# Weight sums and splits one conversion step later, and the last gated output's splits spread over rational steps

## Chip, cores and metric

One core of one Trainium2 chip. The metric is the device time of one execution in microseconds (us): median 962.09 of three runs of the kernel before (962.02 to 962.68).

## What is computed

Inputs and outputs are float32; the weights arrive as 64-bit floats and the kernel turns their bits into float32 itself.

```python
x = attention(q, k, v)               # 2304 tokens x 512, windowed and global
gate = 1.0 / (1.0 + np.exp(-(x @ w_gate)))
val = x @ w_val                      # d_ff 1536
y = gate * val @ w_out
h = y @ w_in                         # d_ff 2048
P = a[0] + a[1] * h + a[2] * h**2 + a[3] * h**3
Q = 1.0 + np.abs(b[0]) * np.abs(h) + np.abs(b[1]) * h**2
out = (P / (Q + 1e-06)) @ w_out2
```

## The kernel before

Three stages follow each other on the core: attention up to about 126 us, the gated layer to about 578 us, the rational layer to the end. Every float32 product is three TensorE matmuls: each operand is split into a high part (a cast on ScalarE) and a low part (a subtraction, on GpSimd for weights), names with `h` and `l`. The 2304 tokens are four tiles of 512 (numbers 0 to 3) and one of 128 (number 4, `glob`); the hidden features come in blocks `f` of 128, twelve of them in the gated layer.

**The passes.** The gated layer first takes tiles 0, 1 and glob in six passes p = 0 to 5, two blocks each (p = 3 takes blocks 6 and 7). In a pass TensorE makes the gate and value products of tile 0, tile 1 and glob (`pg`, `pv`, lines 713 to 715) and the output products (`p`, 831 to 833); at the end glob's gated product is transposed (`turn`, line 785) and split into `gh_glob` (ScalarE, 759) and `gl_glob` (VectorE, 764), and `second_glob` (793 to 799) multiplies both with the output weights: two blocks, lines 797 and 798 with `gh_glob`, 799 with `gl_glob`, each twice. The next pass starts right behind on TensorE.

**The conversion beside it.** During the passes `Weights` converts weights that later parts want, piece by piece, in one order of pieces numbered j: for each block its two gate/value pieces (`v18gv` is block 8 of the gated layer, and there are two of that name; `v19gv` is block 9), for each block an output piece, and pieces of the rational layer (`v20out`, `v21out`, `v20in`; the first digit is the layer). Piece j passes five steps: `magnitude` (ScalarE, two ACTIVATEs, 566 and 567), `bits` (VectorE, three operations, 574 to 576), `add` (GpSimd, 583), `hi` (ScalarE, 605), `lo` (GpSimd, 613), then `keep` writes the result to DRAM (SyncE, 597). `bits` also issues the load of piece j + 3. Three staging buffers `st` of one kind serve all pieces of the rational layer and the sums below.

**The sums.** Tiles 2 and 3 are done after the passes (385 to 567 us) by a Strassen scheme, `strassen`, which wants sums of the weight blocks: `combine` makes them of the two gate/value pieces of a block: 631 (VectorE), 632 (GpSimd), 634 and 636 (VectorE), then two splits (642 on ScalarE, 643 on GpSimd) into two staging buffers, and four writes to DRAM.

**What sets the order.** `Weights.__init__` writes a list per pass, `plan`, of steps with a cost (0.7 or 0.6); `Pace` hands them out between the pieces of TensorE's work in `gated` (919 to 960) until a pass's share is spent. For each j the list has magnitude(j), bits and add of j - 1, hi and lo of j - 2, and, where piece j - 2 was the second of a block, the four parts of `combine` right behind. Each engine works its queue in the order in which the program issues.

**The transition.** The last output products of tiles 2 and 3 (`second` with `final` set) give each m of four a VectorE sum (`gacc`, 845) and at once its split: `yh` (ScalarE, 848) and `yl` (849, GpSimd for m = 0 and 2, VectorE for 1 and 3). The rational layer's pipeline runs over units (unit 0 to 3: tile 0, 4 to 7: tile 2, later tile 3); step n of its loop issues `first` of unit n (`rp`, TensorE 713 to 715), `quad` (GpSimd, 1160) and, for older units, `quot` (VectorE, 1193), `hi` (`rgh`, ScalarE 1202), `lo` (`rgl`, GpSimd 1214) and `second` (TensorE 1243 to 1245, unit n - 4). It calls `before` (the `rest` that `gated` returns) at n = 1 and n = 2; the first call issues tile 2's last output products with their splits, the second tile 3's and then `back(1)`, the loads of tile 1's parked outputs. The table of ln and exp for ScalarE is loaded ahead of the first step (line 1124).

Of the kernel before, what the change touches and what calls it, by code (L numbers as in the profile page):

```python
# [8 lines left out]
F32 = mybir.dt.float32  # L9
# [440 lines left out]
class Weights:  # L450
# [10 lines left out]
    def __init__(self, tc, early, dram, ins, outs):  # L461
# [30 lines left out]
        for p in range(len(ends) - 1):  # L492
            out = []
            last = p == len(ends) - 2
            for j in range(ends[p], ends[p + 1] + (2 if last else 0)):
                for back, steps in ((0, (self.magnitude,)), (1, (self.bits, self.add)), (2, (self.hi, self.lo))):
                    i = j - back
                    if ends[0] <= i < len(self.order):
                        out += [(0.7, step, i) for step in steps]
                        if back == 2 and self.order[i][0] == 1 and self.order[i][2:] == ("gv", 1):  # L500
                            out += [(0.6, self.combine, self.order[i][1], n) for n in range(4)]
# [123 lines left out]
    def combine(self, f, i):  # L625

        nc = self.nc
        v0, v1 = (self.whole[1, f, "gv", k] for k in range(2))
        g0, a0, g1, a1 = v0[:, 0:256], v0[:, 256:512], v1[:, 0:256], v1[:, 256:512]
        if i == 0:  # L630
            nc.vector.tensor_tensor(a1, a0, a1, ALU.add)
            nc.gpsimd.tensor_tensor(a0, g0, a0, ALU.subtract)
        elif i == 1:
            nc.vector.tensor_tensor(g0, a1, g0, ALU.subtract)
        elif i == 2:
            nc.vector.tensor_tensor(g1, g1, g0, ALU.subtract)
        for src, names, turn in ((v0, ("s2", "s3"), 2), (v1, ("s4", "s1"), 3)):
            if i == turn:
                t = self.stage(f"{f}{names[0]}")
                h, l = self.parts(t)  # L640
                src = src.rearrange("p (x c) -> p x c", x=2)
                nc.scalar.copy(h, src)
                nc.gpsimd.tensor_tensor(l, src, h.bitcast(F32), ALU.subtract)
                for x, name in enumerate(names):
                    self.keep((1, f, name, 0), t[:, x * 512 : x * 512 + 512])
# [90 lines left out]
def gated(nc, pools, only, xpool, dram, wp, ident, xh, xl):  # L736
# [85 lines left out]
    def second(f0, i, gs, half):  # L822
# [17 lines left out]
        for m in ms:  # L840
# [5 lines left out]
            if final:  # L846
# [9 lines left out]
                if i > 1:  # L856
                    park(yh[i][:, m], yl[i][:, m])
                else:
                    parks.append(away)
# [250 lines left out]
    def rest():  # L1110
        for _ in range(2):
            queue.pop(0)()
        if not queue:
            back(1)
        wp.pump(len(wp.loads))
# [4 lines left out]
def rational(nc, pools, rest, wp, ident, xh, xl, before, co, out):  # L1120
# [3 lines left out]
    nc.scalar.preload_act_table_set("natural_log_exp_and_others")  # L1124
# [149 lines left out]
    for n in range(len(units) + 8):  # L1274
# [119 lines left out]
```

## Time and profile before

| | |
|---|---|
| median of 3 runs | 962.09 us |
| the profiled execution | 961.38 us, of which the span (first to last instruction) is 959.5 us |
| TensorE busy | 907.8 us (95%) |
| VectorE busy | 753.1 us (78%) |
| ScalarE busy | 581.4 us (61%) |
| GpSimd busy | 572.1 us (60%) |
| mean granted TensorE clock | 0.977 of full speed |

Times in the profile count from the start of the span. PE is TensorE (matmuls), DVE VectorE, ACT ScalarE, POOL GpSimd, SP SyncE. The mean duration of an instruction is what the profiler shows; matmuls overlap, so one that shows 0.39 us starts 0.23 us behind the one before at full clock. A busy share is a mean over stages that differ, so the stages are looked at apart: passes (about 126 to 385 us), Strassen part, transition (566 to 602 us). Idle time of an engine is charged to what ended last before it went on.

### The profile page before, as it was taken

How to read it: one execution, taken by the hardware profiler on the slowest of the kernel's cores; microseconds unless marked ns; L12 is line 12 of the kernel's file. 1: busy time of each engine (PE TensorE's matmuls, PEld its weight loads, DVE VectorE, ACT ScalarE, POOL GpSimd, SP SyncE). 2: the span in 40 equal slices, each digit the busy share in tenths (PEclk: the TensorE clock that was granted, in tenths of full speed). 3: DMA queues.
4: the chain of work that ended last, by engine and by line, in shares of the span. 5: the costliest groups of instructions: out<-in, count | busy, mean ns of one | idle time of the engine just before them, and what ended most of it. 6: DMA issues, size and time to landing. Idle time of an engine off the chain costs nothing.

```text
span 959.5 us, 13769 instructions
## 1 busy us (share of the span) xinstructions
PE 907.8 (95%) x4666; PEld 749.0 (78%) x4666; DVE 753.1 (78%) x1355; ACT 581.4 (61%) x1161; POOL 572.1 (60%) x470
## 2 busy tenths in 40 slices
PE   7989999959797979999999997999999999999998
PEld 6778888848585857788888786888888888888886
DVE  6988885777676777686776848977788889888887
ACT  6978964444444444334444346777777778777673
POOL 4766866657565657346666655635465667566564
PEclk9999999979897989999999999999999999999999
DMA  9755265666565667578989792002200310020112
GB/s 303 235 198 152 78 242 183 239 215 230 192 237 192 225 219 285 208 272 294 328 318 331 268 362 74 0 1 90 86 1 1 111 66 1 1 88 1 45 55 88
DMA packets 60805, 156.24 MB, mean 163 GB/s; under 512 B 7104, under 2 KB 9152, under 8 KB 60736
## 3 DMA queue, kind: packets, MB, share of 16 engines
q1 hardware_dynamic: 60640, 155.24, 46.5%
q8 instruction: 37, 0.61, 0.3%
q14 instruction: 32, 0.26, 0.1%
q10 hardware_dynamic: 96, 0.13, 0.1%
HBM read 103.17 MB, written 52.17 MB: 162 GB/s over the span
## 4 chain that ended last, share of the span: by engine, by line
PE 72%; DVE 13%; POOL 5%; DMA 4%; issue 3%; ACT 2%; SPq 1%; POOLq 0%; DVEq 0%; ACTq 0%
PE rp L1245 6%; PE rp L1243 6%; PE rp L1244 6%; PE rp L715 6%; PE rp L713 6%; PE rp L714 6%; PE p L833 2%; PE p L832 2%; PE p L831 2%; PE pair L261 2%; PE pg L713 2%; PE pg L714 2%; PE pg L715 1%; PE bank L380 1%; PE pv L715 1%
## 5 line engine op out<-in xcount | busy, mean ns | idle before, releaser
L1160 POOL TENSOR_TENSOR v<-v,u 128x512 f32<-128x512 f32 x68 | 91.0, 1338 | 110.5 <-ACT v L1156 110.5
L1214 POOL TENSOR_TENSOR rgl<-t,rgh 128x512 fp32r<-128x512 f32 x64 | 89.9, 1405 | 40.6 <-POOL v L1160 18.8
L1168 DVE TENSOR_TENSOR t<-rp,t 128x512 f32<-128x512 f32 x68 | 46.8, 688 | 45.0 <-ACT t L1164 43.9
L295 POOL TENSOR_TENSOR p<-p,r 128x448 f32<-128x448 f32 x64 | 58.7, 941 | 36.7 <-DVE r L290 24.2
L1153 ACT ACTIVATE u<-rp 128x512 f32<-128x512 f32 x68 | 40.5, 596 | 63.8 <-PE rp L715 60.2
L1193 DVE SCALAR_TENSOR_TENSOR t<-t,co,v 128x512 f32<-128x512 f32 x68 | 72.9, 1072 | 2.4
L1189 DVE SCALAR_TENSOR_TENSOR v<-v,u 128x512 f32<-128x512 f32 x68 | 74.7, 1098 | 0.0
L759 ACT CAST gh<-t 128x512 fp32r<-128x512 f32 x38 | 23.6, 620 | 73.3 <-DVE t L752 64.4
L280 ACT ACTIVATE p<-p,mx 128x224 f32<-128x224 f32 x128 | 60.2, 479 | 7.8 <-DVE mx L272 7.8
L1185 DVE SCALAR_TENSOR_TENSOR v<-v,u 128x512 f32<-128x512 f32 x68 | 59.1, 869 | 1.1 <-ACT u L1181 1.1
L845 DVE TENSOR_TENSOR gacc<-p,gacc 128x512 f32<-128x512 f32 x80 | 51.5, 681 | 10.4 <-PE p L833 10.3
L1156 ACT ACTIVATE v<-u,co 128x512 f32<-128x512 f32 x68 | 55.6, 817 | 2.3
L764 DVE TENSOR_TENSOR gl<-t,gh 128x512 fp32r<-128x512 f32 x38 | 35.5, 934 | 27.2 <-ACT gh L759 27.2
L1177 ACT ACTIVATE u<-v,co 128x512 f32<-128x512 f32 x68 | 49.2, 724 | 6.7 <-POOL v L1160 6.7
L1164 ACT ACTIVATE t<-rp,co 128x512 f32<-128x512 f32 x68 | 51.8, 761 | 0.5 <-POOL rgl L1214 0.5
L1172 DVE SCALAR_TENSOR_TENSOR t<-t,co,rp 128x512 f32<-128x512 f32 x68 | 50.2, 738 | 0.0
L1181 ACT ACTIVATE u<-u,co 128x512 f32<-128x512 f32 x68 | 48.5, 713 | 2.3 <-DVE t L1168 2.2
L1202 ACT CAST rgh<-t 128x512 fp32r<-128x512 f32 x64 | 39.0, 610 | 15.4 <-DVE t L1193 15.4
L272 DVE CUSTOM_DVE_ANT_0 p<-pair,masks 128x224 f32<-128x224 f32 x128 | 42.1, 383 | 7.0 <-DMA masks<-in_masks 6.3
L752 DVE TENSOR_TENSOR t<-pv,t 128x512 f32<-128x512 f32 x28 | 19.2, 685 | 25.8 <-PE pv L715 24.5
L1268 POOL TENSOR_TENSOR racc<-ev,racc 128x512 f32<-128x512 f32 x22 | 37.9, 1743 | 0.0
L261 PE MATMUL pair<-kn,qn 64*128 64x224 f32 x256 | 30.2, 368 | 2.3 <-ACT pgn L319 1.2
(1388 smaller groups left out, 3199.9 us busy)
## 6 DMA issues: line engine op xcount, KB each, us to landing
raw1gv<-in_w_gate_val SPq DMA_DIRECT2D x24, 512.0 KB, 3.7
raw2in<-in_w_in SPq DMA_DIRECT2D x16, 512.0 KB, 4.3
raw2out<-in_w_out SPq DMA_DIRECT2D x16, 512.0 KB, 3.8
kn<-in_k_l SPq DMA_DIRECT2D x15, 448.0 KB, 5.4
raw1out<-in_w_out SPq DMA_DIRECT2D x12, 512.0 KB, 3.6
vn<-in_v_l SPq DMA_DIRECT2D x16, 256.0 KB, 3.8
out<-racc SPq DMA_DIRECT2D x16, 256.0 KB, 2.0
qn<-in_q_l SPq DMA_DIRECT2D x15, 256.0 KB, 4.7
```

The costliest lines, as they stand in the source:

```text
L280: nc.scalar.activation(p, p, AF.Exp, bias=s["mx", half][:, n : n + 1], scale=-1.0, accum_out=s["sm", half][:, n, 0:1])
L295: nc.gpsimd.tensor_tensor(p, p, r, ALU.mult)
L713: nc.tensor.matmul(ps, wh, mh[:, k], start=k == 0, stop=False)
L714: nc.tensor.matmul(ps, wh, ml[:, k], start=False, stop=False)
L715: nc.tensor.matmul(ps, wl, mh[:, k], start=False, stop=k == 3)
L1160: nc.gpsimd.tensor_tensor(s["v"], s["v"], s["u"], ALU.mult)
L1185: nc.vector.scalar_tensor_tensor(s["v"], s["v"], Q_CONST, s["u"], ALU.add, ALU.mult)
L1189: nc.vector.scalar_tensor_tensor(s["v"], s["v"], 2.0, s["u"], ALU.subtract, ALU.mult)
L1193: nc.vector.scalar_tensor_tensor(s["t1"], s["t1"], a0, s["v"], ALU.add, ALU.mult)
L1214: nc.gpsimd.tensor_tensor(s["gl"], s["t1"], s["gh"].bitcast(F32), ALU.subtract)
L1243: nc.tensor.matmul(ps, gh[:, w], wh, start=k == 0, stop=False)
L1244: nc.tensor.matmul(ps, gh[:, w], wl, start=False, stop=False)
```

## The change

Three edits. In the plan of a pass, for each j, hi(j - 2) now comes first, then magnitude(j), bits(j - 1), lo(j - 2), add(j - 1); `combine` is cut in two, `sums` (the four additions) which follows piece j - 3 and `splits` (the two splits with their writes) which follows piece j - 4, each handed out as one item of cost 1.2. In the transition the splits of the last outputs of tiles 2 and 3 are put on the list `parks` instead of being issued; `rest(n)` issues tile 2's output products at n = 1, its four splits at n = 2, tile 3's products at n = 3 and its splits at n = 4 and 5, with `back(1)` at 5. The load of the ln/exp table moves from ahead of the first step to n = 1. The number of instructions stays; lines shift by one (to line 847) and by four or more behind it.

```diff
--- before.py
+++ after.py
@@ -493,12 +493,11 @@
             out = []
             last = p == len(ends) - 2
             for j in range(ends[p], ends[p + 1] + (2 if last else 0)):
-                for back, steps in ((0, (self.magnitude,)), (1, (self.bits, self.add)), (2, (self.hi, self.lo))):
+                for back, steps in ((2, (self.hi,)), (0, (self.magnitude,)), (1, (self.bits,)), (2, (self.lo,)), (1, (self.add,)),
+                                    (3, (self.sums,)), (4, (self.splits,))):
                     i = j - back
-                    if ends[0] <= i < len(self.order):
-                        out += [(0.7, step, i) for step in steps]
-                        if back == 2 and self.order[i][0] == 1 and self.order[i][2:] == ("gv", 1):
-                            out += [(0.6, self.combine, self.order[i][1], n) for n in range(4)]
+                    if ends[0] <= i < len(self.order) and (back < 3 or self.order[i][0] == 1 and self.order[i][2:] == ("gv", 1)):
+                        out += [(1.2 if back > 2 else 0.7, step, i) for step in steps]
             self.plan.append(out)
 
 
@@ -622,27 +621,27 @@
         elif j >= self.EARLY:
             self.keep(key, t)
 
-    def combine(self, f, i):
-
-        nc = self.nc
+    def sums(self, j):
+
+        nc, f = self.nc, self.order[j][1]
         v0, v1 = (self.whole[1, f, "gv", k] for k in range(2))
         g0, a0, g1, a1 = v0[:, 0:256], v0[:, 256:512], v1[:, 0:256], v1[:, 256:512]
-        if i == 0:
-            nc.vector.tensor_tensor(a1, a0, a1, ALU.add)
-            nc.gpsimd.tensor_tensor(a0, g0, a0, ALU.subtract)
-        elif i == 1:
-            nc.vector.tensor_tensor(g0, a1, g0, ALU.subtract)
-        elif i == 2:
-            nc.vector.tensor_tensor(g1, g1, g0, ALU.subtract)
-        for src, names, turn in ((v0, ("s2", "s3"), 2), (v1, ("s4", "s1"), 3)):
-            if i == turn:
-                t = self.stage(f"{f}{names[0]}")
-                h, l = self.parts(t)
-                src = src.rearrange("p (x c) -> p x c", x=2)
-                nc.scalar.copy(h, src)
-                nc.gpsimd.tensor_tensor(l, src, h.bitcast(F32), ALU.subtract)
-                for x, name in enumerate(names):
-                    self.keep((1, f, name, 0), t[:, x * 512 : x * 512 + 512])
+        nc.vector.tensor_tensor(a1, a0, a1, ALU.add)
+        nc.gpsimd.tensor_tensor(a0, g0, a0, ALU.subtract)
+        nc.vector.tensor_tensor(g0, a1, g0, ALU.subtract)
+        nc.vector.tensor_tensor(g1, g1, g0, ALU.subtract)
+
+    def splits(self, j):
+
+        nc, f = self.nc, self.order[j][1]
+        for k, names in enumerate((("s2", "s3"), ("s4", "s1"))):
+            t = self.stage(f"{f}{names[0]}")
+            h, l = self.parts(t)
+            src = self.whole[1, f, "gv", k].rearrange("p (x c) -> p x c", x=2)
+            nc.scalar.copy(h, src)
+            nc.gpsimd.tensor_tensor(l, src, h.bitcast(F32), ALU.subtract)
+            for x, name in enumerate(names):
+                self.keep((1, f, name, 0), t[:, x * 512 : x * 512 + 512])
 
     def allow(self, n):
         self.limit += n
@@ -853,10 +852,7 @@
                     park(t[:, 0:512], t[:, 512:1024])
                     wp.keep((9, i, "y", m), t)
 
-                if i > 1:
-                    park(yh[i][:, m], yl[i][:, m])
-                else:
-                    parks.append(away)
+                parks.append((lambda m=m, park=park: park(yh[i][:, m], yl[i][:, m])) if i > 1 else away)
         if half == 1 and i in (1, 3):
             for g in range(G):
                 wp.release((1, f0 + g, "out", 0))
@@ -1107,12 +1103,13 @@
         step()
     pace.finish()
 
-    def rest():
-        for _ in range(2):
+    def rest(n):
+        for _ in range({1: 2, 3: 2}.get(n, 0)):
             queue.pop(0)()
-        if not queue:
+        for _ in range({2: 4, 4: 2, 5: 2}.get(n, 0)):
+            parks.pop(0)()
+        if n == 5:
             back(1)
-        wp.pump(len(wp.loads))
 
     return yh, yl, rest
 
@@ -1121,7 +1118,6 @@
     G = G2
     NF = FF2 // 128
     acc = [None] * len(TILES)
-    nc.scalar.preload_act_table_set("natural_log_exp_and_others")
     nc.vector.tensor_scalar_mul(co[:, 0:4], co[:, 0:4], -1.0)
     nc.scalar.activation(co[:, 4:6], co[:, 4:6], AF.Abs)
     nc.vector.memset(co[:, 6:7], Q_CONST * LN_SCALE)
@@ -1272,6 +1268,8 @@
     steps = dict(first=first, abs=abs_, lin=lin, quad=quad, p3=p3, p2=p2, p1=p1, log=log, exp=exp, r1=r1, r2=r2,
                  quot=quot, hi=hi, lo=lo, second=second, out=evacuate)
     for n in range(len(units) + 8):
+        if n == 1:
+            nc.scalar.preload_act_table_set("natural_log_exp_and_others")
         for name, ahead, *args in PLAN2:
             u = n + ahead
             if name in ("second", "out") and u >= LATER:
@@ -1286,8 +1284,7 @@
                 if i == LAST_TURNS[-1] and name == "first" and fs[0] % G == G - 1:
                     for k in range(4):
                         wp.release((2, fs[0] - G + 1, "in", k))
-        if n in (1, 2):
-            before()
+        before(n)
         wp.pump(len(wp.loads))
```

How the instructions move, at three places.

ScalarE at the end of pass 3, where `gh_glob` stands (`hi` of a piece is a CAST at 605 before, 604 now; splits of sums are `st8s`, `st9s`); before:

```order
L605 CAST w19gv_0_3147<-v19gv_2977 128x2x256
L566 ACTIVATE v21out_3152<-raw2out_3048 128x512
L567 ACTIVATE q21out_3153<-raw2out_3048 128x512
L605 CAST w19gv_0_3162<-v19gv_3041 128x2x256
L642 CAST st9s_3189<-v19gv_2977 128x2x256
L642 CAST st9s_3196<-v19gv_3041 128x2x256
L566 ACTIVATE v18out_3203<-raw1out_3111 128x512
L567 ACTIVATE q18out_3204<-raw1out_3111 128x512
L605 CAST st20out_3229<-v20out_3104 128x512
L759 CAST gh_glob<-pt_3231 128x256
```

and now:

```order
L604 CAST w19gv_0_3138<-v19gv_3043 128x2x256
L565 ACTIVATE v21out_3140<-raw2out_3050 128x512
L566 ACTIVATE q21out_3141<-raw2out_3050 128x512
L641 CAST st8s_3155<-v18gv_2933 128x2x256
L641 CAST st8s_3162<-v18gv_2948 128x2x256
L604 CAST st20out_3185<-v20out_3060 128x512
L565 ACTIVATE v18out_3187<-raw1out_3095 128x512
L566 ACTIVATE q18out_3188<-raw1out_3095 128x512
L604 CAST st21out_3220<-v21out_3140 128x512
L758 CAST gh_glob<-pt_3222 128x256
```

Between the last `w19gv` cast and `gh_glob` stood block 9's two sums splits; now block 8's stand there, and the cast `st21out`, which stood behind `gh_glob`, is ahead of it.

GpSimd in the same stretch (583 and 582 are `add`, 613 and 612 `lo`, 632 and 630 the sums' subtraction, 643 and 642 the splits); before:

```order
L613 TENSOR_TENSOR w19gv_0_3147<-v19gv_2977,w19gv_0_3147 128x2x256
L583 TENSOR_TENSOR v20out_3104<-v20out_3104,q20out_3105 128x512
L613 TENSOR_TENSOR w19gv_0_3162<-v19gv_3041,w19gv_0_3162 128x2x256
L632 TENSOR_TENSOR v19gv_2977<-v19gv_2977 128x256
L643 TENSOR_TENSOR st9s_3189<-v19gv_2977,st9s_3189 128x2x256
L643 TENSOR_TENSOR st9s_3196<-v19gv_3041,st9s_3196 128x2x256
L583 TENSOR_TENSOR v21out_3152<-v21out_3152,q21out_3153 128x512
L613 TENSOR_TENSOR st20out_3229<-v20out_3104,st20out_3229 128x512
L583 TENSOR_TENSOR v18out_3203<-v18out_3203,q18out_3204 128x512
L613 TENSOR_TENSOR st21out_3292<-v21out_3152,st21out_3292 128x512
```

and now:

```order
L630 TENSOR_TENSOR v18gv_2933<-v18gv_2933 128x256
L612 TENSOR_TENSOR w19gv_0_3138<-v19gv_3043,w19gv_0_3138 128x2x256
L582 TENSOR_TENSOR v20out_3060<-v20out_3060,q20out_3061 128x512
L642 TENSOR_TENSOR st8s_3155<-v18gv_2933,st8s_3155 128x2x256
L642 TENSOR_TENSOR st8s_3162<-v18gv_2948,st8s_3162 128x2x256
L612 TENSOR_TENSOR st20out_3185<-v20out_3060,st20out_3185 128x512
L582 TENSOR_TENSOR v21out_3140<-v21out_3140,q21out_3141 128x512
L630 TENSOR_TENSOR v19gv_2995<-v19gv_2995 128x256
L612 TENSOR_TENSOR st21out_3220<-v21out_3140,st21out_3220 128x512
L582 TENSOR_TENSOR v18out_3187<-v18out_3187,q18out_3188 128x512
L642 TENSOR_TENSOR st9s_3283<-v19gv_2995,st9s_3283 128x2x256
```

The subtraction of block 8's sums now comes behind the add of `v19gv`, its splits behind the add of `v20out`; the add of `v21out`, which the cast `st21out` needs, comes behind these splits and the `lo` of `st20out`; block 9's splits go to the next pass.

GpSimd at the transition, from the first rational `quad` on; before:

```order
L1160 TENSOR_TENSOR v_5756<-v_5756,u_5754 128x512
L1160 TENSOR_TENSOR v_5779<-v_5779,u_5777 128x512
L849 TENSOR_TENSOR yl_5802<-gacc_4266,yh_5801 128x512 x2
L1160 TENSOR_TENSOR v_5848<-v_5848,u_5846 128x512
L849 TENSOR_TENSOR yl_5874<-gacc_4421,yh_5873 128x512 x2
L1214 TENSOR_TENSOR rgl_5855<-t_5758,rgh_5854 128x512
L1160 TENSOR_TENSOR v_5935<-v_5935,u_5933 128x512
```

and now:

```order
L1156 TENSOR_TENSOR v_5755<-v_5755,u_5753 128x512
L1156 TENSOR_TENSOR v_5779<-v_5779,u_5777 128x512
L1156 TENSOR_TENSOR v_5840<-v_5840,u_5838 128x512
L848 TENSOR_TENSOR yl_5802<-gacc_4266,yh_5801 128x512 x2
L1210 TENSOR_TENSOR rgl_5847<-t_5757,rgh_5846 128x512
L1156 TENSOR_TENSOR v_5879<-v_5879,u_5877 128x512
L1210 TENSOR_TENSOR rgl_5886<-t_5781,rgh_5885 128x512
L1156 TENSOR_TENSOR v_5948<-v_5948,u_5946 128x512
L848 TENSOR_TENSOR yl_5905<-gacc_4421,yh_5904 128x512
L1210 TENSOR_TENSOR rgl_5971<-t_5842,rgh_5970 128x512
```

Tile 3's two splits (`yl_5874`) stood ahead of the first `rgl`; now only tile 2's two do, and tile 3's (`yl_5905`) come behind the second `rgl`.

## Rows read from the trace of the kernel before

**Rows 1.** Windows: PE, PEld, DVE, ACT, POOL busy (count); granted clock; DMA share; GB/s.
```profile
265.00:305.00 40.00, 33.45 (x146) 27.04 (x145) 28.33 (x42) 16.99 (x31) 25.52 (x21) 0.87 0.64 224
...
385.00:425.00 40.00, 39.97 (x177) 32.71 (x178) 29.44 (x37) 14.06 (x25) 16.39 (x12) 1.00 0.61 220
580.00:620.00 40.00, 35.09 (x148) 28.54 (x147) 37.69 (x45) 29.95 (x48) 22.46 (x16) 0.96 0.09 27
```

**Rows 2.** Waits of PE over the whole span: us in total, times, longest.
```profile
PE p_glob L797 <- ACT gh_glob L759: 27.8, 4, 9.5
PE rp L1245 <- POOL rgl L1214: 4.9, 1, 4.9
```

**Rows 3.** Timeline of PE, ends of passes 1, 3, 5: start, duration, instruction, [idle before <- releaser].
```profile
204.31 0.79 PE L799 MATMUL p_glob<-w12out,gl_glob 128*128 128x512 f32 x1 [0.47 <-DVE gl_glob L764]
...
295.05 0.79 PE L797 MATMUL p_glob<-w16out,gh_glob 128*128 128x512 f32 x1 [6.08 <-ACT gh_glob L759]
...
296.73 0.80 PE L799 MATMUL p_glob<-w16out,gl_glob 128*128 128x512 f32 x1 [0.46 <-DVE gl_glob L764]
...
298.61 0.63 PE L713 MATMUL pg<-xh,w18gv 128*128 128x512 f32 x1
...
385.03 0.50 PE L799 MATMUL p_glob<-w110out,gl_glob 128*128 128x512 f32 x1 [2.27 <-DVE gl_glob L764]
```

**Rows 4.** Windows right behind three waits of PE, for the granted clock.
```profile
298.50:302.00 3.50, 3.50 (x10) 2.66 (x10) 3.03 (x5) 1.76 (x3) 0.75 (x2) 0.51 0.61 241
385.00:388.00 3.00, 2.97 (x13) 2.48 (x14) 2.31 (x3) 1.14 (x2) 2.03 (x2) 1.00 0.93 373
595.00:598.00 3.00, 2.97 (x8) 2.33 (x9) 2.96 (x4) 2.14 (x4) 1.72 (x2) 0.58 0.03 5
```

**Rows 5.** Timeline of ACT at the end of pass 3.
```profile
291.94 1.14 ACT L642 CAST st9s<-v19gv 128x512 fp32r<-128x512 f32 x2 [5.56 <-DVE v19gv L634]
...
294.63 0.37 ACT L759 CAST gh_glob<-pt 128x256 fp32r<-128x256 f32 x1
```

**Rows 6.** Timeline of DVE in pass 3.
```profile
273.78 0.69 DVE L576 SCALAR_TENSOR_TENSOR v19gv<-raw1gv,v19gv 128x512 uint32<-128x512 uint32 x1
...
278.74 0.42 DVE L752 TENSOR_TENSOR t_glob<-pgv,t_glob 128x256 f32<-128x256 f32 x1
...
286.44 0.43 DVE L575 TENSOR_SCALAR v20out<-v20out 128x512 uint32<-128x512 uint32 x1
...
294.24 1.38 DVE L575 TENSOR_SCALAR v21out<-v21out 128x512 uint32<-128x512 uint32 x1
...
296.26 0.42 DVE L764 TENSOR_TENSOR gl_glob<-pt,gh_glob 128x256 fp32r<-128x256 f32 x1
```

**Rows 7.** Timeline of POOL in pass 3.
```profile
279.55 2.86 POOL L643 TENSOR_TENSOR st8s<-v18gv,st8s 128x512 fp32r<-128x512 f32 x2 [1.19 <-ACT st8s L642]
...
287.67 1.30 POOL L583 TENSOR_TENSOR v20out<-v20out,q20out 128x512 uint32<-128x512 uint32 x1 [1.55 <-PE pv L715]
...
290.73 0.72 POOL L632 TENSOR_TENSOR v19gv<-v19gv 128x256 f32<-128x256 f32 x1 [0.54 <-DMA raw1out<-in_w_out]
```

**Rows 8.** Timeline of PE at the transition.
```profile
595.03 0.50 PE L1245 MATMUL rp<-w20out,rgl 128*128 128x512 f32 x1 [4.91 <-POOL rgl L1214]
```

**Rows 9.** Timeline of ACT at the transition.
```profile
568.63 1.28 ACT L1124 ACT_TABLE_LOAD   x1
...
586.36 0.62 ACT L1202 CAST rgh<-t 128x512 fp32r<-128x512 f32 x1 [1.08 <-DVE t L1193]
...
591.34 1.22 ACT L848 CAST yh<-gacc 128x512 fp32r<-128x512 f32 x2 [1.96 <-DVE gacc L845]
```

**Rows 10.** Timeline of POOL at the transition.
```profile
592.03 1.27 POOL L849 TENSOR_TENSOR yl<-gacc,yh 128x512 fp32r<-128x512 f32 x1 [1.88 <-ACT yh L848]
593.26 1.72 POOL L1214 TENSOR_TENSOR rgl<-t,rgh 128x512 fp32r<-128x512 f32 x1
```

**Rows 11.** Timeline of DVE at the transition.
```profile
584.66 1.67 DVE L1193 SCALAR_TENSOR_TENSOR t<-t,co,v 128x512 f32<-128x512 f32 x1
```

## Prediction

> **What bounds the kernel now.** First the windows by stage. In the Strassen part TensorE is busy 39.97 of 40 us at full clock; in a pass only 33.45 of 40, at a granted clock of 0.87, and around the transition 35.09 [rows 1]. No other engine is full in the passes (DVE 28.33, POOL 25.52), so TensorE waits there for a chain of short steps, not for a busy engine. Second, the waits of TensorE: 27.8 us for `gh_glob` in four passes and 4.9 us for the first `rgl` [rows 2]; at most a few us elsewhere. Third, what each wait costs besides itself: behind 6.08 us of waiting for `gh_glob`, the 3.5 us from 298.5 show a clock of 0.51 (its lower level, 1.2 GHz) and 10 matmuls, while the 3 us behind the 2.27 us wait at 385.03 show 1.00 (2.4 GHz) and 13; behind the 4.91 us wait at the transition it is 0.58 and 8 in 3 us [rows 3, 4]. So a long wait costs about two us more than it lasts, and a wait of 2.27 us nothing more.
>
> Fourth, what `gh_glob` waits for. On ScalarE it starts at 294.63 without idle time ahead: the splits `st9s` came at 291.94 after 5.56 us of waiting for the sums of block 9, then two ACTIVATEs and the cast `st20out` [rows 5]. The sums wait for GpSimd's subtraction at 290.73, which stands behind the add of `v20out` (287.67) and a `lo` [rows 7]. `gl_glob` is 296.26, behind the bits of `v21out` on VectorE [rows 6], and releases line 799 at 296.73 [rows 3]. From line 799 on TensorE has no more waits, so the start of 799 sets where the next pass begins.
>
> **Part 1, the plan of the passes.** It removes no instruction; per pass the same steps are issued, the writes to DRAM and loads included. What I walk is the order of the change in pass 3 with durations of the rows, from a point that both orders share: the end of bits of the first `v19gv`, 273.78 + 0.69 = 274.5 [rows 6].
> - Now the add of this piece (1.3, as 287.67 [rows 7]) ends at 275.8, the cast 0.5 and magnitude(`v20out`) 1.15 behind it stand ahead of glob's sigmoid, and VectorE's `t_glob` starts at 277.9, against 278.74 [rows 6]: 0.8 earlier, since no sums stand ahead of it.
> - Then bits of the second `v19gv`, 1.6 with GpSimd idle; `t_1` and `gl_1` with the cast between, 2.0; sums of block 8, 0.42 + 0.73 + 0.8 with the subtraction between [rows 7]; bits of `v20out`, 2.5: they end at 286.4 instead of 287.6, 1.2 earlier.
> - GpSimd: add 1.3 (287.7), splits `st8s` 2.7 (between 2.5 and 2.86 [rows 7]), `lo` of `st20out` 1.25, add of `v21out` 1.3: 293.0. VectorE's bits of `v21out` have four us of cover there. The cast `st21out` 0.5, then `gh_glob` at 293.5, against 294.63 [rows 5]: 1.1 earlier, although a cast more stands ahead of it.
> - `gl_glob` no longer has bits ahead of it, but sums of block 9, whose subtraction comes behind the add of `v21out`: 293.0 + 0.7 + 0.8 = 294.5, against 296.26 [rows 6]. Line 799 then starts at about 295.1, 1.2 behind 797 as TensorE's two matmuls at half clock take it there, against 296.73 [rows 3]: 1.6 earlier.
>
> The same walk carried from the start of a pass gives 2.6, as GpSimd and VectorE collide less in its first half. I take 2.1 for each of passes 2 to 4. Pass 1 takes over one group of sums and splits from pass 0, whose share no longer reaches it; its walk gives 202.9 for line 799 against 204.31 [rows 3]: 1.4. In pass 5 only the 2.27 us wait for `gl_glob` can go; bits of `v24in` leave VectorE's queue ahead of it, a cast of `st24in` enters ScalarE's: 1.2. Pass 0 does not change. Sum 1.4 + 3 x 2.1 + 1.2 = **8.9**. TensorE still waits some four us in passes 1 to 4, so I give nothing back for the clock; that is the low side's room.
>
> Bounds: nothing at all at one end; at the other all that the waits cost. That is 27.8 + 2 for `gh_glob` and its `gl_glob`, 2.27, and some 2.3 of slow matmuls for each of four passes (5 fewer in 3.5 us [rows 4], and 6 or so ahead of them): 41.
>
> What waits newly: the split buffers are three, and the four writes of the sums now fall together with those of `st20out` and `st21out`; ScalarE's split stands ahead of the sigmoid of the next tile. TensorE needs that sigmoid only for its output products one tile later, so this is covered by more than 5 us of matmuls.
>
> **Part 2, the transition.** TensorE stops at 590.1 for 4.91 us [rows 8], since `rgl` of unit 0 is made at 593.26 behind tile 3's `yl` at 592.03 on GpSimd [rows 10], and this behind `yh` at 591.34 [rows 9] and tile 3's sums. In the new order only tile 2's two `yl` are ahead of it. VectorE: four sums of tile 2 from 576.9 to 579.5, two operations 1.3, `quot` 1.67 to 582.5, against 584.66 + 1.67 [rows 11], as four low parts no longer stand ahead. Then `rgh` 583.1, four `yh` to 585.3, two `yl` to 586.5, `rgl` 1.72 to 588.2. TensorE, with the same work ahead, would ask at 590.1: the wait goes. With it go the slow matmuls behind it, 5 fewer in 3 us and two or three later, 1.6 us [rows 4]. Late next is tile 3's sums, which now free TensorE's accumulators some us later: 0.5 back. Tile 2's `yh` and `yl` are wanted by unit 4 at about 586.8, a margin of one us or less. **6.0**; between 2.3, all that VectorE has idle in 40 us there (37.69 busy [rows 1]), and 6.5.
>
> **Part 3, the table.** It took 1.28 us at 568.63, the next operation right behind at 569.92 [rows 9], while the first `rp` was still running. Now it stands ahead of the first logarithm, 1.3 us on the way to `quot` and `rgl` of unit 0: at worst 589.5 instead of 588.2, still before 590.1. Nothing, and 0 to 1.3 if the margin is gone.
>
> **Sum.** 961.38 - 8.9 - 6.0 = 946.5 for an execution like the profiled one, which lies 0.7 below the median: 947.
>
> **Rivals.**
> - *The passes give nothing, the transition does.* `gh_glob` has four GpSimd operations in a row ahead of it, and one slow one eats the 1.1 us. 961.4 - 6.0 + 0.7 = 956. For it: `gh_glob` moves only 1.1 us in my walk.
> - *The conversion leaves TensorE's path.* If both halves of the pass get shorter, waits under about two us cost no clock either [rows 3, 4], and nearly all of the 41 goes: about 915 with the transition. Against it: DVE and POOL are busy 28.33 and 25.52 of 40 [rows 1] and hinder each other.
> - *The transition's wait comes back a few units later*, as VectorE is busy 37.69 of 40 [rows 1]: 2.3 instead of 6.0, 951.
> - *Slower: the new chain in its slow form.* The same VectorE operation takes 0.43 beside an idle GpSimd and 1.38 beside a busy one [rows 6]. If bits of the second `v19gv` and of `v20out` take 3.5, `gl_1` 1.5, the splits 2.86 and each of `lo` and add 1.8, line 799 comes at 300 instead of 296.73: 3.3 in each of five passes, 16.5 lost, 6.0 won, 972. It decides from line 799 later than 298.0 (five times 1.2 is the transition's gain). Against it: in the new order the sums and the splits come while VectorE has other things, and GpSimd's total is the same. The Trainium skill (SBUF — State Buffer, section "Who interferes with whom") speaks for it: the pair of ports that VectorE and GpSimd share is an exclusive lock, and the loser blocks for a whole instruction. By that rule each of the chain's five GpSimd operations could be held up by one of VectorE's, and the time would be this rival's. The trace agrees that they block each other, by 0.95 us in the rows named.
>
> **How the numbers follow.** The forecast has 0.60, passes without gain 0.16, the conversion off the path 0.07, the wait that comes back 0.05, all gains given back 0.04, slower 0.08. A measurement of this kernel tells about 0.2% (1.9 us) from no change. Faster: 0.60 + 0.16 + 0.07 + 0.05 = 0.88; same 0.04; slower 0.08. The range goes from 932 (passes at twice my gain, with the slow matmuls of some of them gone) to 958 (passes without gain, transition a little less): left out are 0.07 + 0.04 + 0.08 = 0.19.
>
> **What would show it.** Right: the wait of line 797 for `gh_glob` falls to 4 to 5 us in passes 2 to 4, and that of line 799 is below 0.5; line 799 of pass 5 waits about one us; line 1245 has no wait near 590 and the clock there is 1.00; `rgl` of unit 0 ends near 588. Wrong: `gh_glob` later behind `pv` than 6.1 us, with the cast `st21out` waiting for the add of `v21out`; TensorE waiting for `rgl` or accumulators between 590 and 620; a wait of unit 4 for `yl`.

## The result: 1.1% slower

The changed kernel takes 973.06 us (median of 4 runs, 971.29 to 975.07) against 962.38 before: ratio 1.0112, 95% interval 1.009 to 1.0133. The forecast was 947, the range 932 to 958.

TensorE's idle times in the changed kernel, all over 0.6 us between the end of pass 0 and 650 us (timeline of PE: start, duration, instruction, [idle before <- releaser]; lines are one lower than before up to 847, four lower in the rational layer):

```profile
180.88 0.80 PE L712 MATMUL pg<-xh,w12gv 128*128 128x512 f32 x1 [3.88 <-ACT t L750]
206.64 0.80 PE L796 MATMUL p_glob<-w12out,gh_glob 128*128 128x512 f32 x1 [6.22 <-ACT gh_glob L758]
209.10 0.79 PE L798 MATMUL p_glob<-w12out,gl_glob 128*128 128x512 f32 x1 [1.25 <-DVE gl_glob L763]
255.22 0.80 PE L796 MATMUL p_glob<-w14out,gh_glob 128*128 128x512 f32 x1 [6.93 <-ACT gh_glob L758]
257.69 0.79 PE L798 MATMUL p_glob<-w14out,gl_glob 128*128 128x512 f32 x1 [1.25 <-DVE gl_glob L763]
303.44 0.80 PE L796 MATMUL p_glob<-w16out,gh_glob 128*128 128x512 f32 x1 [6.91 <-ACT gh_glob L758]
305.91 0.79 PE L798 MATMUL p_glob<-w16out,gl_glob 128*128 128x512 f32 x1 [1.25 <-DVE gl_glob L763]
351.45 0.80 PE L796 MATMUL p_glob<-w18out,gh_glob 128*128 128x512 f32 x1 [6.93 <-ACT gh_glob L758]
353.93 0.79 PE L798 MATMUL p_glob<-w18out,gl_glob 128*128 128x512 f32 x1 [1.26 <-DVE gl_glob L763]
398.05 0.80 PE L796 MATMUL p_glob<-w110out,gh_glob 128*128 128x512 f32 x1 [5.59 <-ACT gh_glob L758]
476.59 0.50 PE L976 MATMUL pb<-txh,w15g 128*128 128x512 f32 x1 [0.65 <-DVE s L991]
607.46 0.50 PE L1239 MATMUL rp<-w20out,rgh 128*128 128x512 f32 x1 [1.12 <-DVE gacc L844]
643.71 0.66 PE L1205 MATMUL rt<-ident,t 128*128 128x128 f32 x4 [0.99 <-DVE t L1189]
```

These answer to [rows 3] and [rows 8]. In passes 2 to 4 the waits for `gh_glob` did not fall to four us, they rose from 6.1 to 6.9, and those for `gl_glob` rose from 0.46 to 1.25. Pass 1 has a new wait for a sigmoid, 3.88 us, while its wait for `gh_glob` fell from 9.5 to 6.2; pass 5 has a new wait for `gh_glob`. The 4.91 us of the transition became 1.12. Two more lines of before are wanted to follow line 799 (now 798) pass by pass:

```profile
250.04 0.79 PE L799 MATMUL p_glob<-w14out,gl_glob 128*128 128x512 f32 x1 [0.46 <-DVE gl_glob L764]
...
343.96 0.79 PE L799 MATMUL p_glob<-w18out,gl_glob 128*128 128x512 f32 x1 [0.45 <-DVE gl_glob L764]
```

| first start of line 799 (798) | before | after | late by | of which in this pass |
|---|---|---|---|---|
| pass 1 | 204.31 | 209.10 | 4.8 | 4.3 |
| pass 2 | 250.04 | 257.69 | 7.7 | 2.9 |
| pass 3 | 296.73 | 305.91 | 9.2 | 1.5 |
| pass 4 | 343.96 | 353.93 | 10.0 | 0.8 |
| pass 5 | 385.03 | 399.08 | 14.1 | 4.1 |

Half a us of the lateness was there before pass 1, at the end of pass 0 (156.74 against 156.21). A single pass is not exact to better than 1.4 us: `x1` below, whose passes are those of before, has 47.1, 45.8 and 46.7 us for passes 2 to 4 where the kernel before has 45.7, 46.7 and 47.2. Their sum is steady, 139.6 and 139.7, and here it is 144.8: 5.2 lost in passes 2 to 4.

Tile 2's last output products begin at 586.46 instead of 570.47, 16.0 late (slow matmuls behind pass 5 and waits in the Strassen part, 0.65 us the longest, make the rest); the span is 971.8 instead of 959.5, 12.3 late. So the passes lost 16.0 and the transition gave 3.7.

Where pass 3 lost, aligned at the start of line 799 of the pass before (250.04 and 257.69), VectorE first (same columns):

```profile
273.13 1.80 DVE L575 SCALAR_TENSOR_TENSOR v18gv<-raw1gv,v18gv 128x512 uint32<-128x512 uint32 x1
...
282.66 0.69 DVE L575 SCALAR_TENSOR_TENSOR v19gv<-raw1gv,v19gv 128x512 uint32<-128x512 uint32 x1
286.79 0.43 DVE L751 TENSOR_TENSOR t_glob<-pgv,t_glob 128x256 f32<-128x256 f32 x1 [3.44 <-ACT t_glob L750]
...
301.25 1.50 DVE L629 TENSOR_TENSOR v19gv<-v19gv,v19gv 128x256 f32<-128x256 f32 x1
303.59 1.48 DVE L631 TENSOR_TENSOR v19gv<-v19gv,v19gv 128x256 f32<-128x256 f32 x1 [0.84 <-POOL v19gv L630]
305.10 0.43 DVE L632 TENSOR_TENSOR v19gv<-v19gv,v19gv 128x256 f32<-128x256 f32 x1
305.44 0.42 DVE L763 TENSOR_TENSOR gl_glob<-pt,gh_glob 128x256 fp32r<-128x256 f32 x1
```

then GpSimd:

```profile
273.08 1.30 POOL L612 TENSOR_TENSOR w17out<-v17out,w17out 128x512 fp32r<-128x512 f32 x1 [0.73 <-ACT w17out L604]
...
295.48 1.28 POOL L582 TENSOR_TENSOR v20out<-v20out,q20out 128x512 uint32<-128x512 uint32 x1 [2.35 <-DVE v20out L575]
296.72 2.86 POOL L642 TENSOR_TENSOR st8s<-v18gv,st8s 128x512 fp32r<-128x512 f32 x2
299.54 1.71 POOL L612 TENSOR_TENSOR st20out<-v20out,st20out 128x512 fp32r<-128x512 f32 x1
301.21 1.26 POOL L582 TENSOR_TENSOR v21out<-v21out,q21out 128x512 uint32<-128x512 uint32 x1
```

and ScalarE:

```profile
272.38 0.62 ACT L604 CAST w17out<-v17out 128x512 fp32r<-128x512 f32 x1 [3.12 <-POOL v17out L582]
...
302.50 0.62 ACT L604 CAST st21out<-v21out 128x512 fp32r<-128x512 f32 x1 [3.96 <-POOL v21out L582]
303.02 0.36 ACT L758 CAST gh_glob<-pt 128x256 fp32r<-128x256 f32 x1
```

In the first half, `lo` (line 612) now starts in the middle of bits: 273.08 beside 273.13, and the third operation of bits takes 1.80 instead of 0.69. A cast (272.38) waits 3.12 us for an add of GpSimd, and `magnitude` of a later piece stands behind it. Bits of the first `v19gv` end at 283.35, 25.7 behind the alignment, against 24.4 before [rows 6]: 1.2 late. The end of the pass: splits, `lo` and add take 5.8 where 5.25 was counted, and the cast `st21out` waits 3.96 us for this add, with `gh_glob` right behind it: the sign of being wrong that the prediction names. Block 9's sums run at 1.5 us where 0.42 was counted, with `gl_glob` behind them at 305.44.

### The profile page after: what moved, and what is told of

The parts are those of the page before. It is cut to its first block, busy times and chain, and to the rows that moved or that the text cites. A ratio compares the mean times of both kernels' runs of the same rounds, so it can differ in the third digit from the quotient of the medians.

```text
span 971.8 us, 13780 instructions
## 1 busy us (share of the span) xinstructions
PE 912.9 (94%) x4666; PEld 752.1 (77%) x4666; DVE 765.8 (79%) x1355; ACT 580.7 (60%) x1161; POOL 573.1 (59%) x470
## 4 chain that ended last, share of the span: by engine, by line
PE 73%; DVE 13%; POOL 4%; DMA 4%; issue 3%; ACT 2%; SPq 1%; POOLq 0%; ACTq 0%; DVEq 0%
PE rp L1239 5%; PE rp L1240 5%; PE rp L1241 5%; PE rp L714 5%; PE rp L713 5%; PE rp L712 5%; PE p L832 3%; PE p L830 3%; PE p L831 3%; PE pair L261 2%; PE pg L712 2%; PE pg L713 2%; PE pg L714 2%; PE pv L714 2%; PE pv L712 2%
## 5 line engine op out<-in xcount | busy, mean ns | idle before, releaser
L1210 POOL TENSOR_TENSOR rgl<-t,rgh 128x512 fp32r<-128x512 f32 x64 | 90.6, 1415 | 40.8 <-issue 18.7
L295 POOL TENSOR_TENSOR p<-p,r 128x448 f32<-128x448 f32 x64 | 58.6, 940 | 37.3 <-DVE r L290 24.8
L1164 DVE TENSOR_TENSOR t<-rp,t 128x512 f32<-128x512 f32 x68 | 46.7, 687 | 41.0 <-ACT t L1160 39.8
L1160 ACT ACTIVATE t<-rp,co 128x512 f32<-128x512 f32 x68 | 51.8, 762 | 2.6 <-POOL rgl L1210 2.6
L763 DVE TENSOR_TENSOR gl<-t,gh 128x512 fp32r<-128x512 f32 x38 | 32.3, 849 | 20.8 <-ACT gh L758 20.8
```

The lines of the kernel that those rows point to most:

```text
L295: nc.gpsimd.tensor_tensor(p, p, r, ALU.mult)
L1210: nc.gpsimd.tensor_tensor(s["gl"], s["t1"], s["gh"].bitcast(F32), ALU.subtract)
```

## Experiments

All are timed against the kernel before on the same chip. I give the theory first: **the new order of the items does the harm (VectorE and GpSimd now run into each other, ScalarE's casts wait for GpSimd ahead of sigmoids, pass 5 runs out of staging buffers), the late sums do little, and the transition gains what it can.** The first rival: the late sums, with `gl_glob` behind them, are the cost.

### The two stages apart

`x1`, the transition alone: the plan and `combine` as before, the rest as changed. `x2`, the plan alone.

```diff
@@ x1, on the changed kernel @@
-for back, steps in ((2, (self.hi,)), (0, (self.magnitude,)), (1, (self.bits,)), (2, (self.lo,)), (1, (self.add,)), (3, (self.sums,)), (4, (self.splits,))):
+for back, steps in ((0, (self.magnitude,)), (1, (self.bits, self.add)), (2, (self.hi, self.lo))):
...
@@ x2, on the changed kernel @@
-parks.append((lambda m=m, park=park: park(yh[i][:, m], yl[i][:, m])) if i > 1 else away)
+if i > 1:
+    park(yh[i][:, m], yl[i][:, m])
+else:
+    parks.append(away)
...
```

> Edit: the plan of the passes as before, the splits of the last outputs and the table load as changed. Theory (the passes lose, the transition gains): read off the two traces, the changed kernel is 16.0 us late when tile 2's last output products begin and 12.3 us late at the end, so the transition gives 3.7 us: about 958.7 against 962.4. Rival (the transition's gain of 6.0 of my prediction was cut short by what the plan leaves behind): about 956.4. Rival (the gain shows only because the passes came late): 962.4, no change. In the profile: no wait of line 1241 for rgl, a wait of about 1.1 us for accumulators ahead of the first second, and in the passes the waits of the kernel before (9.5, 6.1, 6.1, 6.1, 2.3).

Measured: 959.64 us, ratio 0.9962 (0.9947 to 0.9977), 3.7 us faster.

> Edit: the plan of the passes as changed, the transition as before. Theory: the plan alone costs what the changed kernel was late by at the transition, 15 to 16 us: about 978. Rival (part of that comes with the transition's edits): below 974. In the profile: waits for gh_glob of 6.2, 6.9, 6.9, 6.9 and 5.6 us, for a sigmoid 3.9 us in pass 1, and 4.9 us for the first rgl.

Measured: 978.48, ratio 1.0152 (1.0132 to 1.0173), 14.7 us slower. The two add up: 1.0152 x 0.9962 = 1.0113, the change has 1.0112. The transition's smaller gain is its own, as `x1`'s timeline of PE shows:

```profile
594.50 0.50 PE L1240 MATMUL rp<-w20out,rgh 128*128 128x512 f32 x1 [1.12 <-DVE gacc L845]
630.75 0.66 PE L1206 MATMUL rt<-ident,t 128*128 128x128 f32 x4 [0.95 <-DVE t L1190]
```

The wait for `rgl` is gone, and 1.12 us for accumulators (tile 3's sums) and 0.95 for a VectorE result 36 us later come in.

### The plan's edit in its parts

`x3`: the new order of items, sums undivided behind `lo`. `x4`: the sums and splits late, the old order of items. `x5`: only `hi` ahead of `magnitude`. `x6`: only `lo` ahead of `add`.

```diff
@@ on the kernel before @@
-for back, steps in ((0, (self.magnitude,)), (1, (self.bits, self.add)), (2, (self.hi, self.lo))):
@@ x3 @@
+for back, steps in ((2, (self.hi,)), (0, (self.magnitude,)), (1, (self.bits,)), (2, (self.lo,)), (1, (self.add,))):
@@ x4 @@
+for back, steps in ((0, (self.magnitude,)), (1, (self.bits, self.add)), (2, (self.hi, self.lo)), (3, (self.sums,)), (4, (self.splits,))):
@@ x5 @@
+for back, steps in ((2, (self.hi,)), (0, (self.magnitude,)), (1, (self.bits, self.add)), (2, (self.lo,))):
@@ x6 @@
+for back, steps in ((0, (self.magnitude,)), (1, (self.bits,)), (2, (self.hi, self.lo)), (1, (self.add,))):
...
```

> Edit: only the new order of a step's items (hi, magnitude, bits, lo, add); the sums and splits stay undivided right behind lo. Theory (lo now runs on GpSimd beside bits on VectorE, which lengthens bits by 1.1 to 1.4 us in the first half of a pass): each of passes 1 to 4 loses 1 to 1.5 us there, and pass 1 has the new wait for a sigmoid of about 3.9 us with its slow matmuls, since the cast ahead of the sigmoid waits for the add; together 966 to 972. Rival (the order of items is harmless, the late sums do it all): 962 within 1.5.

Measured: 974.48, ratio 1.0105 (1.0084 to 1.0127), 10.1 us: the order of the items does most of the harm, more than I gave it. TensorE waits 9.1 us for `gh_glob` in each of passes 2 to 4; the wait for a sigmoid in pass 1 is 1.10 us and not the 3.9 expected.

> Edit: only the sums one step later and their splits two, the order of the other items as before, so the cast of st21out stays behind gh_glob and the casts ahead of it wait for one add less. Theory (in the change gh_glob is late because the cast of st21out with the add, the lo and the splits of GpSimd before it stands ahead): here gh_glob comes 2 to 4 us earlier behind the last pv than in the kernel before, gl_glob still comes behind the sums of block 9; 952 to 960. Rival (the late sums are what costs, through gl_glob behind them and through block 3's sums in pass 1): 966 to 975.

Measured: 963.13, ratio 0.9996 (0.998 to 1.0012): neither the theory's gain nor the rival's loss. It loses in pass 1, where TensorE waits 2.34 us for an accumulator that VectorE's gated product frees, and line 796 comes at 207.21 instead of 202.62 (797 before), and gains in passes 3 and 4, whose periods from line 796 to 796 are 45.3 and 44.9 us instead of 46.7 and 47.2:

```profile
181.77 0.50 PE L712 MATMUL pv<-xh,w12gv 128*128 128x512 f32 x1 [2.34 <-DVE t L751]
207.21 0.80 PE L796 MATMUL p_glob<-w12out,gh_glob 128*128 128x512 f32 x1 [9.65 <-ACT gh_glob L758]
253.41 0.80 PE L796 MATMUL p_glob<-w14out,gh_glob 128*128 128x512 f32 x1 [5.86 <-ACT gh_glob L758]
298.74 0.79 PE L796 MATMUL p_glob<-w16out,gh_glob 128*128 128x512 f32 x1 [5.83 <-ACT gh_glob L758]
343.63 0.79 PE L796 MATMUL p_glob<-w18out,gh_glob 128*128 128x512 f32 x1 [5.89 <-ACT gh_glob L758]
```

My expectation of a gain of several us from an earlier `gh_glob` was wrong: it stayed where it was, within 0.3 us.

> Edit on the kernel before: only the cast hi(j-2) goes ahead of magnitude(j) on ScalarE; GpSimd keeps add(j-1) ahead of lo(j-2), the sums stay behind lo. Theory (the run with both orders lost 10 us because the lo and the splits stand ahead of the add on GpSimd, so that lo runs beside bits and the cast of st20out waits for a late add): this half alone costs little, 961 to 966. Rival (the cast, which waits for GpSimd's add, holds magnitude and the sigmoids behind it on ScalarE, and that is the cost): 969 to 975, with waits for a sigmoid.

Measured: 973.28, ratio 1.0095 (1.0063 to 1.0126). The theory, that this half is nearly free, falls.

> Edit on the kernel before: only lo(j-2), with the sums behind it, goes ahead of add(j-1) on GpSimd; on ScalarE magnitude(j) stays ahead of hi(j-2). Theory: this half carries the loss of the run with both: 969 to 976, with waits for gh_glob of 8 us and more in passes 2 to 4, the cast of st20out ahead of it waiting some 3.7 us for the add of v20out. Rival: 961 to 966.

Measured: 969.31, ratio 1.0058 (1.0033 to 1.0083), at the low end of what the theory gave it; the waits for `gh_glob` are 7.2 us in passes 2 to 4, where 8 and more were expected. The page's busy times tell the two halves apart. Before, `x5` and `x6`:

```profile
PE 907.8 (95%) x4666; PEld 749.0 (78%) x4666; DVE 753.1 (78%) x1355; ACT 581.4 (61%) x1161; POOL 572.1 (60%) x470
```
```profile
PE 913.7 (94%) x4666; PEld 753.0 (77%) x4666; DVE 753.4 (77%) x1355; ACT 583.3 (60%) x1161; POOL 573.1 (59%) x470
```
```profile
PE 912.6 (94%) x4666; PEld 752.9 (78%) x4666; DVE 766.7 (79%) x1355; ACT 583.5 (60%) x1161; POOL 578.2 (60%) x470
```

With `lo` first VectorE's same 1355 instructions take 13.6 us longer, and with the whole change 12.7 (765.8); with `hi` first nothing is added. So it is `lo` first that lets VectorE and GpSimd collide more. That the longer busy time is what costs is not shown: in `x4` it is 758.8 at no loss, and in `x11` below 769.3 in a faster kernel. The lengths of the passes, read off the traces from the first start of line 799 in one pass to that in the next (798 where the lines are shifted), say where each part loses:

| us | pass 1 | passes 2 to 4 | pass 5 |
|---|---|---|---|
| before | 48.1 | 139.7 | 41.1 |
| `x1`, the same passes | 48.1 | 139.6 | 42.4 |
| the change | 52.4 | 144.8 | 45.2 |
| `x3`, new order | 49.4 | 144.9 | 44.0 |
| `x4`, late sums | 51.8 | 136.4 | 40.8 |
| `x5`, `hi` first | 48.7 | 141.6 | 46.5 |
| `x6`, `lo` first | 47.8 | 140.3 | 43.4 |

In pass 1 the late sums lose 3.7 by themselves and the new order 1.3. In passes 2 to 4 the new order loses as much as the whole change; the late sums gain 3.2 there with the old order and nothing with the new one. So "the late sums do little" holds for their total alone. Neither half of the new order makes its loss of 5.3 in passes 2 to 4: `hi` first loses 2.0, `lo` first 0.7. Most of what `x6` loses lies elsewhere, in pass 5 and behind it: from line 799 of pass 5 to the first output product of the rational layer it takes 210.8 us instead of 204.5, with the clock at 0.50 in the first four us and four waits of 0.45 to 0.67 us for VectorE in the Strassen part.

`hi` first costs in another way. Its timeline of PE has waits for `gh_glob` of 6.4 us in passes 2 to 4 (6.1 before), a sigmoid's 1.10 in pass 1 and, where before there was none, this in pass 5:

```profile
393.37 0.80 PE L797 MATMUL p_glob<-w110out,gh_glob 128*128 128x512 f32 x1 [5.92 <-ACT gh_glob L759]
```

### Pass 5 and the staging buffers

ScalarE in pass 5 of the changed kernel:

```profile
389.06 0.62 ACT L847 CAST sty<-gacc 128x512 fp32r<-128x512 f32 x1 [4.24 <-DVE gacc L844]
389.58 0.62 ACT L604 CAST st24in<-v24in 128x512 fp32r<-128x512 f32 x1
...
394.60 0.62 ACT L847 CAST sty<-gacc 128x512 fp32r<-128x512 f32 x1 [3.27 <-DMA k24in<-st24in]
397.11 0.62 ACT L847 CAST sty<-gacc 128x512 fp32r<-128x512 f32 x1 [1.89 <-DMA k90y<-sty]
397.64 0.36 ACT L758 CAST gh_glob<-pt 128x256 fp32r<-128x256 f32 x1
```

The cast `st24in` at 389.58 stood behind `gh_glob` before. It takes one of the three buffers; the next two parked splits `sty` then wait for writes to DRAM, and `gh_glob` behind them. `x9` gives pass 5 of the changed kernel the old order; `x12` gives pass 5 of the kernel before the cast ahead of `magnitude`.

```diff
@@ x9, on the changed kernel @@
+new = ((2, (self.hi,)), (0, (self.magnitude,)), (1, (self.bits,)), (2, (self.lo,)), (1, (self.add,)))
+old = ((0, (self.magnitude,)), (1, (self.bits, self.add)), (2, (self.hi, self.lo)))
+for back, steps in (old if p == 5 else new) + ((3, (self.sums,)), (4, (self.splits,))):
@@ x12, on the kernel before @@
+for back, steps in (((2, (self.hi,)), (0, (self.magnitude,)), (1, (self.bits, self.add)), (2, (self.lo,))) if p == 5 else
+                    ((0, (self.magnitude,)), (1, (self.bits, self.add)), (2, (self.hi,)), (2, (self.lo,)))):
...
```

> Edit on the changed kernel: in pass 5 alone the items of a step stand in the order of the kernel before (magnitude, bits, add, hi, lo), so that the third cast st24in comes behind the parked output splits sty and behind gh_glob; late sums, the other passes and the transition stay. Theory (pass 5 lost 4 to 5 us of the change's loss, since that cast takes one of three staging buffers and a sty then waits for a buffer's write to DRAM ahead of gh_glob): 4 to 5.5 us below the changed kernel, 967.5 to 969.5, the wait of line 797 in pass 5 below 1.5 us, gl_glob's about 2.3. Rival (the buffers are late because the conversion as a whole is late): within 1.5 of 973.

Measured: 967.43, ratio 1.0037 (1.0025 to 1.005), against 1.0112 with the whole change: 5.6 us less by the medians, 7.2 by the ratios, more than the 4 to 5.5 expected. Of this the trace shows 3.4 in pass 5, which takes 41.7 us from line 799 to 799 (352.04 to 393.75) instead of 45.2, and no slow matmuls behind it (a clock of 1.00 in the next 5.9 us, where the changed kernel has 0.80). The waits of pass 5 are 0.66 and 1.87:

```profile
391.14 0.50 PE L797 MATMUL p_glob<-w110out,gh_glob 128*128 128x512 f32 x1 [0.66 <-ACT gh_glob L759]
393.75 0.50 PE L799 MATMUL p_glob<-w110out,gl_glob 128*128 128x512 f32 x1 [1.87 <-DVE gl_glob L764]
```

> Edit on the kernel before: only in pass 5 the cast hi(j-2) goes ahead of magnitude(j); all else as before. Theory (this alone puts the third cast st24in into the ring of three staging buffers ahead of the parked splits, so that they and gh_glob behind them wait for writes to DRAM): 4 to 6 us slower, 967 to 969.5, line 797 in pass 5 waiting 4.5 to 6 us for gh_glob where it did not wait before. Rival (it takes the late conversion of the other passes too): within 1.5 of the kernel before.

Measured: 967.65, ratio 1.0049 (1.0032 to 1.0066), 4.7 us slower, with the same picture on ScalarE (the last `sty` waits 4.18 us for a write):

```profile
382.76 0.62 ACT L849 CAST sty<-gacc 128x512 fp32r<-128x512 f32 x1 [1.30 <-DMA k24in<-st24in]
387.56 0.62 ACT L849 CAST sty<-gacc 128x512 fp32r<-128x512 f32 x1 [4.18 <-DMA k90y<-sty]
388.09 0.36 ACT L760 CAST gh_glob<-pt 128x256 fp32r<-128x256 f32 x1
```

So about half of what `hi` first costs is one cast in one pass, with the other passes left alone.

### Is it data that TensorE waits for, or a place in a queue?

`x7` moves `turn` alone; `x8` adds the transition, `x10` does it on the changed kernel, `x11` on the transition with late sums and the old order of items.

```diff
@@ x7, on the kernel before @@
+gg = None
 for half in pending:
     half()
+    if gg is None:
+        gg = turn(f0, t)
     spot(L)
-gg = turn(f0, t)
```

> Edit on the kernel before: glob's transposes with the split into gh_glob and gl_glob are issued between the two halves of tile 0's output products instead of behind them, so gh_glob stands ahead of the splits of sums and the cast of st20out on ScalarE, and gl_glob ahead of the sums and of bits of v21out on VectorE. Theory (TensorE waits only for gh_glob's place in ScalarE's queue, not for data): the waits of line 797 go from 6.1 to under 1 us in passes 2 to 4; the conversion, whose steps still take their time, then holds the pass elsewhere (a sigmoid behind the casts), so the pass shortens by 2 to 6 us: 935 to 955. Rival (the conversion alone sets the length of a pass, wherever TensorE waits): the wait of 6 us moves to a sigmoid and the time stays within 959 to 965.

Measured: 948.25, ratio 0.9838 (0.9807 to 0.9869). Line 797 no longer waits for `gh_glob` in any pass; in pass 3 TensorE waits for `t_glob` ahead of the transposes and half a us for an accumulator, and then, in pass 4, for a sigmoid. Behind pass 5 a new wait for VectorE comes in:

```profile
274.05 0.44 PE L789 MATMUL pt<-ident,t_glob 128*128 128x128 f32 x2 [0.72 <-DVE t_glob L752]
283.18 0.47 PE L797 MATMUL p_glob<-w16out,gh_glob 128*128 128x512 f32 x1 [0.50 <-DVE gacc L845]
290.13 0.50 PE L713 MATMUL pv<-xh,w18gv 128*128 128x512 f32 x1 [2.20 <-ACT t L751]
...
376.73 1.10 PE L813 MATMUL pty<-ident,gacc 128*128 128x128 f32 x4 [3.03 <-DVE gacc L806]
```

Passes 3 and 4 take 43.4 us each (239.80 to 283.18 to 326.56 at line 797) instead of 46.7 and 47.2. No wait over 2.4 us is left in passes 1 to 5, and as in [rows 4] the clock stays up behind them: behind the longest, 2.36 us at 230.67, it is 1.00 in 3.3 us. Behind the 3.03 us at 376.73 it is 0.52 in 2.3 us.

> Edit on the kernel before: the transition's edits of the change and the early transposes together. Theory (the two stages are apart and their gains add): 3.7 us below the run with the early transposes alone, within 1.5. Rival: no gain beyond it.

Measured: 943.86, ratio 0.979 (0.9761 to 0.982): the gains add (4.4 below `x7`), and this is the best kernel of the study, 2.1% faster than before.

> Edit on the changed kernel: glob's transposes and split between the two halves of tile 0's output products, as in the run that gained 1.6% on the kernel before. Theory (the new order lengthens the chain of the conversion through the first half of a pass and in pass 5, which stays when TensorE no longer waits for gh_glob's place): above the run with transition and early transposes on the old plan by 6 to 12 us, 950 to 956. Rival (the plan's loss came only through gh_glob's and gl_glob's places): 942 to 946.

Measured: 958.96, ratio 0.9948 (0.9931 to 0.9964), 15 us above `x8`; the theory's direction, and more than it gave. With `gh_glob` out of the way, the new order's own waits show, twice in each of passes 2 to 4 (3.1 to 3.4 and 1.8 to 2.6 us); in pass 4:

```profile
297.30 0.50 PE L712 MATMUL pv<-xh,w18gv 128*128 128x512 f32 x1 [3.38 <-ACT t L750]
316.72 0.80 PE L712 MATMUL pg<-xh,w18gv 128*128 128x512 f32 x1 [2.63 <-ACT t L750]
```

> Edit on the kernel before: the transition, the early transposes and the late sums and splits (the order of the other items as before). Theory (with the sums late, the waits of TensorE for t_glob and for a sigmoid that the early transposes leave, 2 us each, shrink, since no splits stand ahead of the sigmoids; but in pass 1 block 3's sums come in): 938 to 945 against about 944. Rival (the late sums in pass 1 cost what they did alone, some 4 us, and nothing is left to gain in passes 2 to 4): 945 to 950.

Measured: 949.59, ratio 0.985 (0.9827 to 0.9874): the rival. The late sums cost 5.7 us here against `x8`; TensorE waits for a sigmoid 5.05 us in pass 2 and 4.25 in each of passes 3 to 5 (2.2 in `x7`), and in pass 1 it waits 2.35 for an accumulator, as in `x4`. In pass 4:

```profile
294.68 0.80 PE L712 MATMUL pv<-xh,w18gv 128*128 128x512 f32 x1 [4.25 <-ACT t L750]
```

## Why the prediction was wrong

- **What bounds the kernel** was right: the waits for `gh_glob` and the slow matmuls behind them. `x7` takes them away and gets 1.62%, some 15.6 us.
- **Part 1, the shared starting point.** The plan was to win 8.9 us and lost 14.7 (`x2`). The step that failed first: "from a point that both orders share: the end of bits of the first `v19gv`". They do not share it. In the half of the pass ahead of it, which the walk leaves out, `lo` now runs beside bits and casts wait for adds ahead of `magnitude`, and the point comes 1.2 us later (1.4 in the mean of passes 2 to 4: 25.7 behind line 799 against 24.3). I had added 0.5 us a pass for this half, "as GpSimd and VectorE collide less in its first half"; they collide more, 12.7 us in all of VectorE's busy time. How much of the delay is the collision stays open: in the same mean the point is at 24.0 in `x6`, which has it too (a third operation of bits of 1.77 beside `lo`), at 24.8 in `x5` and at 25.0 in `x3`.
- **Part 1, the walk itself.** From that point to the end of bits of `v20out` I gave 11.9 us and the trace has 12.0; the errors in it cancel. From there to `gh_glob` I gave 7.1 and it took 7.6, as the splits and `lo` took 4.5 of GpSimd instead of 3.95. `gl_glob` was put 1.0 behind `gh_glob`; it comes 2.4 behind, since the two sums on VectorE took 1.5 each beside GpSimd's operations and not 0.42. Together with the starting point that makes 1.5 lost where 1.6 was to be won at line 799.
- **Part 1, pass 1.** I forecast 1.4 won, and 4.3 was lost. Here the sigmoid of the next tile (180.25 on ScalarE) stood behind a cast that waited 3.44 us for an add of GpSimd, and TensorE waited 3.88 us for it. "This is covered by more than 5 us of matmuls" was the claim on sigmoids that failed. The late sums have the larger share: `x4` loses 3.7 in this pass, with a wait of 2.34 for an accumulator, and `x3` 1.3, with a wait of 1.10 for the sigmoid. The 3.88 comes with both.
- **Part 1, pass 5.** I forecast 1.2 won and put the cast `st24in` down as harmless; 4.1 was lost at line 799. I named the three buffers and priced their waits at nothing, although in the kernel before a `sty` already waited 1.22 us for a write there. `x12` prices it: 4.7 us.
- **Part 2, the transition**: the mechanism was right, the wait for `rgl` is gone, but 3.7 came instead of 6.0. The accumulators' wait measured 1.12 and not 0.5, and 0.95 us came back at 630.75 as a wait for VectorE (busy 3.96 of the 4 us around it), the small beginning of the rival that I gave 0.05. These are 1.6 of the 2.3 us that are missing; the rest is not placed, and lies within the interval of `x1` (2.2 to 5.1 us gained).
- **Part 3, the table**: nothing of it shows in TensorE's waits; it was not tried alone.
- **The rival that came true** was the slower one, at 972, to which I gave 0.08. Its mechanism is there in part: bits and sums ran in their slow form. But it gave 3.3 us to each of five passes, and passes 2 to 4 lost 5.2 together, not by the slow form alone (`x6`), while passes 1 and 5 lost 4 each by other means, so its number was met by chance. The Trainium skill (SBUF — State Buffer, section "Who interferes with whom") says that VectorE and GpSimd share a pair of ports under an exclusive lock, which blocks one of them for the other's whole instruction. The rows are in keeping with it: the same bits operation takes 0.69 alone and 1.80 beside `lo`.

Still open: how the two halves of the order together lose 5.3 us in passes 2 to 4, where each alone loses 2.0 or less; and the parts of the plan's edit do not add up (`x4`, `x5` and `x6` give 1.0149 together against 1.0152 for `x2`, yet `x5` and `x6` give 1.0153 where `x3`, which has both, measured 1.0105).

## What to carry to other kernels

A reordering that removes no instruction can cost more than the wait that it aims at: on an in-order engine, look first at what waits in front of the operation that another engine wants, and move that operation (one transpose and its cast gained 1.6% here) before moving everything around it. When steps of two engines that hinder each other are shifted by a step, walk the whole period, not the part from a point that looks shared, and compare the parts of the edit pass by pass: a total near zero (`x4`) can hide a loss in one pass and a gain in others. A ring of buffers that is already waited for once is a bound: count who takes a buffer between two waits.

## What the runs showed of the hardware

VectorE's busy time is not a property of its instructions: 1355 of them took 753.1 us or 766.7 us by the order on GpSimd alone, with single operations at 0.42 and 1.50 or at 0.69 and 1.80. And a clock that falls behind waits of 6 us stayed up when they were cut to waits of about 2 us each: with early transposes the granted clock of the whole execution is 0.989 (0.977 before, 0.968 with the change). Waits of that length are not safe wherever they stand: in `x6`, where 0.90 and 2.39 us stand three us apart at the end of pass 5, the clock was 0.50 in the four us behind them.
